# Warming products on a constant of ones, and three row transfers moved to GpSimd's queue

## The chip, the cores and the metric

One core of a Trainium2 chip runs the kernel. The time is the device time of one execution in microseconds, as the median of several runs. The profile is of one more execution of the same program.

## The reference

The inputs are x (2048 rows of 512), weights for an attention branch A and for a feed-forward branch B, and a gate vector. All is float32.

```
g = sigmoid(sum(x * gate_w, -1))
# A: linear attention, 32 heads of 16
q, k, v = split(x @ wqkv)
pq, pk = per head q @ w_phi, k @ w_phi
phi(p) = concat(softmax(p), softmax(-p))          # 32 features a head
kv = sum over rows of phi(pk)^T v;  z = sum over rows of phi(pk)
a = (phi(pq) kv / (phi(pq) z + 1e-6)) @ wo
# B: feed-forward, 1792 hidden
h = relu(x @ w1 + b1)^2
b = h @ w2 + b2
out = g * a + (1 - g) * b
```

## The kernel before

Every float32 product is made of three TensorE products of split operands: each operand is a high part (ScalarE copies it, rounded) and a low part (VectorE subtracts), as `split` (line 62) makes them, and `mm3` and `block` issue high by high and the two mixed terms.

The feed-forward branch sets the rhythm. The 14 hidden chunks are done in two sweeps of seven over four blocks of 512 rows; each step of the work list issues one `up` (12 products of 512 columns) and the `down` products of an earlier step. All other work is hung on slots between them: `at(slot, f, ...)` puts a function into a slot, two whole slots to a step, some 5 us each in the first sweep. The scheduler may issue ready work sooner; `tc.issue_after(ins)` pins what is traced in it behind `ins` in the order of that engine's queue, without a wait.

Start: `warm_up` (485) clears a tile `zeros` on VectorE and issues ten products of it into a PSUM bank that nobody reads; `start` (495) then fetches x's first block in four chunks and the weights of three hidden chunks, splits them and issues the first 36 true products in a fixed order (line 552). A first tiny ScalarE activation (`ready`, 521) reads `zeros` too.

The k and v projections of attention run in the first sweep as eight pairs of row chunks, one pair from slot 14 + 4.5 p on (`pair_steps`, 651), by a scheme of seven block products in place of eight. For pair p, `sums_load` (593) fetches two tiles of rows, 256 KB each and in runs of 512 bytes; `sums_add` (604) makes four sums in place, on GpSimd except for the first pair; `sums` (614) splits the result on ScalarE and VectorE. The weights of three of the seven blocks do not fit: they are kept in DRAM (`wkeep`) and come back in turn, 512 KB at a time, into three slots (two tiles `sloto`, one `slotez`), on ScalarE's queue (`again`, 626, issue shown as line 635) as soon as the products that read a slot are done.

`x_load` (564) fetches the next block's rows in four tiles of 256 KB, `x_split` (579) splits them later. These tiles and the halves of `sums_load` share one set of four buffers (`stage`, tag "in"), given out in the order of the code; a transfer waits until the low part of the tile that had the buffer before is made. Block 2 comes on GpSimd's queue, blocks 1, 3 and the return to block 0 (b = 4) on SyncE's through `load` (85). The halves of pair 4 (counted from 0) come on GpSimd's queue, all others on SyncE's.

GpSimd's queue holds, in the first sweep: writing the kept weights, part results to DRAM (901), some of the gate's row tiles (263), block 2's rows (570), the halves for pair 4 (600) and the additions (609 to 612). `st["summed"]` is the last of the latest additions, `st["stored"]` the latest store or halves' transfer behind which the next additions are pinned; `st["ahead"]` is the latest of SyncE's halves, behind which the gate's row tiles for blocks 2 and 3 are pinned.

Of the kernel before, what the change touches and what calls it, by code (L numbers as in the profile page):

```python
# [10 lines left out]
AF = mybir.ActivationFunctionType  # L11
# [5 lines left out]
P = 128  # L17
S, D, H, DH, F = 2048, 512, 32, 16, 1792
NK = D // P
SB = 512  # L20
NB = S // SB
# [14 lines left out]
def tile_gated_mix(ctx: ExitStack, tc: tile.TileContext, xT, xn, wqT, wkT, wphi, wv, wo, w1, b1, w2, b2, gw, out):  # L36
    nc = tc.nc
# [6 lines left out]
    work = pool("work", 2)  # L44
# [5 lines left out]
    def used(p):  # L50
        banks.remove(p)
        banks.append(p)
# [32 lines left out]
    def load(src, eng=nc.sync):  # L85
        t = stage.tile([P, 512], F32, tag="in", name="in")
        st["in"] = eng.dma_start(t, src)
        return t

    def row():  # L90
        return work.tile([P, D], F32, tag="row", name="row", bufs=6)

    def ffn_tiles(nm, fc):
        return (fpool.tile([P, 512], F32R, tag=nm + "h", name=f"{nm}h{fc}"),
                fpool.tile([P, 512], F32R, tag=nm + "l", name=f"{nm}l{fc}"))
# [25 lines left out]
    st, up_w, down_w = {}, {}, {}  # L121
# [137 lines left out]
    def gate_load(n):  # L259
        eng, pin = ((nc.sync, "in" if n > 1 else "wv"), (nc.gpsimd, "summed"), (nc.sync, "ahead"), (nc.sync, "ahead"))[n // NC]  # L260
        st["xn", n] = row()
        with tc.issue_after(st[pin].ins):
            st["xrow"] = eng.dma_start(st["xn", n], xn[n])
# [151 lines left out]
    def hidden(fc, ps):  # L415
        r = work.tile([P, SB], F32, tag="r", name="r")
        with tc.high_priority(offset=AHEAD):
            st["relu"] = nc.scalar.activation(r, ps, AF.Relu, bias=b1c[:, fc:fc + 1])  # L418
        nc.scalar.activation(r, r, AF.Square)  # L419
        hh = work.tile([P, SB], F32R, tag="hh", name="hh", bufs=LAG + 1)  # L420
        hl = work.tile([P, SB], F32R, tag="hl", name="hl", bufs=LAG + 1)
        st["act"] = split(r, hh, hl, nc.scalar, nc.vector)
        st["dve"] = st["lo"]
        return hh, hl
# [52 lines left out]
    def do_w1(fc):  # L477
        up_w[fc] = by_k(load_ffn("w1", w1[fc], fc))
# [4 lines left out]


    def warm_up():
        z = st["zeros"] = work.tile([P, 512], mybir.dt.bfloat16, tag="r", name="zeros")
        nc.vector.memset(z, 0.0)
        st["warm"] = ps_a.tile([P, 512], F32, tag="s", name="warm")
        idle(10)

    def idle(n):
        for _ in range(n):
            st["up"] = nc.tensor.matmul(st["warm"], st["zeros"][:, :P], st["zeros"], start=True, stop=True)


    def start():
        fs, wide = range(FIRST), FIRST * P
        W = [ffn_tiles("w1", f) for f in fs]
        ps = [p.tile([P, SB], F32, tag="s", name="u") for p in (ps_e, ps_b, ps_f)]
        xs = st["x", 0] = []  # L500
        for f in fs:
            up_w[f] = [tuple(z[:, P * f:P * (f + 1)] for z in W[k]) for k in range(NK - 1)]
            up_w[f].append(tuple(z[:, wide:] for z in W[f]))
        raw = [(stage.tile([P, 512], F32, tag="in", name="in"), row()) for _ in range(NK)]
        last = act = None

        def fetch(dst, src):
            nonlocal last
            with tc.issue_after(last.ins) if last else nullcontext():
                last = nc.sync.dma_start(dst, src)  # L510

        def first_w(k, a, b):
            return (raw[k][1][:, a * P:b * P].rearrange("p (f c) -> p f c", f=b - a),
                    w1[a:b, :, k * P:(k + 1) * P].rearrange("f p c -> p f c"))

        def follow(i, eng, *a):
            with tc.issue_after(i.ins) if i else nullcontext():
                return eng(*a)

        ready = small.tile([P, 1], F32, tag="den", name="ready", bufs=2)  # L520
        act = follow(nc.scalar.dma_start(*first_w(0, 0, 1)), nc.scalar.activation, ready, st["zeros"][:, :1], AF.Copy)
        for k in range(NK):
            fetch(raw[k][0], xT[0, :, k, :])
            fetch(*first_w(k, 0 if k else 1, FIRST))
        dve = None
        for k in range(NK):
            u, t = raw[k]
            xh, xl = (xpool.tile([P, SB], F32R, tag=g, name=f"{g}0_{k}") for g in ("xh", "xl"))
            xs.append((xh, xl))
            if k == 0:  # L530
                w = [(t[:, a:b], *(z[:, a:b] for z in W[k])) for a, b in ((0, P), (P, wide))]
            elif k < NK - 1:
                w = [(t[:, :wide], *(z[:, :wide] for z in W[k]))]
            else:
                w = [(t[:, P * f:P * (f + 1)], *(z[:, wide:] for z in W[f])) for f in fs]
            if k < 2:
                dve = follow(dve, nc.vector.tensor_copy, xh, u)
            else:
                act = follow(act, nc.scalar.activation, xh, u, AF.Copy)
            for src, hi, lo in w:  # L540
                act = follow(act, nc.scalar.activation, hi, src, AF.Copy)
            lows = [(lo, src, hi.bitcast(F32), ALU.subtract) for src, hi, lo in w]
            lows.insert(k == 0, (xl, u, xh.bitcast(F32), ALU.subtract))
            for x in lows:
                dve = follow(dve, nc.vector.tensor_tensor, *x)
            terms = [(f, 0, xh) for f in fs] + [(f, 0, xl) for f in fs] + [(f, 1, xh) for f in fs]
            if k == 0:
                terms.insert(1, terms.pop(6))
            if k == NK - 1:
                terms.sort(key=lambda x: x[0])  # L550
            for n, (f, part_, x) in enumerate(terms):
                st["up"] = follow(st["up"], lambda: nc.tensor.matmul(
                    ps[f], up_w[f][k][part_], x, start=k == 0 and (part_, x) == (0, xh),
                    stop=k == NK - 1 and part_ == 1))
        fetch(b1c, b1)
        do_w1(FIRST)
        for f in fs:
            hid[f] = hidden(f, ps[f])
            if f == 0:
                st["act0"] = st["act"]  # L560
        for p in (ps_e, ps_b, ps_f):
            used(p)

    def x_load(b):
        if b == 2:
            st["xin", b] = []
            for k in range(NK):
                with tc.issue_after(st["summed"].ins):
                    t = stage.tile([P, 512], F32, tag="in", name="in")
                    st["summed"] = nc.gpsimd.dma_start(t, xT[b, :, k, :])  # L570
                    st["xin", b].append(t)
                if k > 1:
                    gate_load(NC + k)
                    st["summed"] = st["xrow"]
        else:
            st["xin", b] = [load(xT[b % NB, :, k, :]) for k in range(NK)]
        st["x", b] = []

    def x_split(b, k):
# [13 lines left out]
    def sums_load(p):  # L593
        b, c = ROWS[p]
        rows = xT[b].rearrange("p k (h c r) -> p k h c r", h=2, c=2)[:, :, :, c, :]
        st["rows", p] = [stage.tile([P, 2, 2, P], F32, tag="in", name="in") for _ in range(2)]
        for i, t in enumerate(st["rows", p]):
            if p == 4:
                with tc.issue_after(st["stored"].ins):
                    st["stored"] = nc.gpsimd.dma_start(t, rows[:, 2 * i:2 * i + 2])  # L600
            else:
                st["ahead"] = nc.sync.dma_start(t, rows[:, 2 * i:2 * i + 2])
# [191 lines left out]
    for b in range(NB):  # L794
        for c in range(NC):
            s = b * SL + 2.5 * c - 1 if b > 1 else 17.5 + c / 2 if b else max(5.5, 3.5 + 2 * c)
            if b != 1 or c < 2:
                at(s, gate_load, b * NC + c)
            at(s + (4.5 if b == 1 else 3), gate_chunk, b * NC + c)
        if c == NC - 1:  # L800
            at(s + 4.5 if b == 1 else s + 3, gates, b)
        s, late = ((4, 2), (19.5, 1), (22, 2.5), (36, 2))[b]
        at(s, x_load, b + 1)
        for k in range(NK):
            at(s + late + k / 2, x_split, b + 1, k)
# [19 lines left out]
    for p in range(NB * NC // 2):  # L825
        n, s = 2 * p, 56.5 + 6 * p
        q, late = divmod(n, NC)[0], p == NB * NC // 2 - 1
# [31 lines left out]
    at(2, rows_alike, gwb, gw)  # L859
    at(2, rows_alike, b2b, b2)  # L860
    warm_up()
    start()
    with tc.issue_after(st["act0"].ins):
        for fc in range(LAG + 1):
# [84 lines left out]
```

## Time and profile before

| | |
|---|---|
| median of 3 runs | 507.90 us (507.86 to 508.17) |
| the profiled execution's own time | 508.57 us |
| its span, first to last instruction | 506.8 us |
| TensorE busy | 502.0 us, 99% |
| VectorE, ScalarE, GpSimd busy | 405.9, 256.2, 88.4 us |
| moved by DMA | 76.13 MB, 150 GB/s on the mean |

Product ends are modelled, so a busy share of 99% hides small stalls. They are seen in the distance between the starts of neighbouring products. In rows of the timeline the columns are start, duration, engine, line, operation, tile written and read, and in brackets the idle time before, with what ended it. A queue is marked with a q: SPq is SyncE's, ACTq ScalarE's; GpSimd's issues are shown as POOL DMA_DIRECT2D.

### The profile page before, as it was taken

How to read it: one execution, taken by the hardware profiler on the slowest of the kernel's cores; microseconds unless marked ns; L12 is line 12 of the kernel's file. 1: busy time of each engine (PE TensorE's matmuls, PEld its weight loads, DVE VectorE, ACT ScalarE, POOL GpSimd, SP SyncE). 2: the span in 40 equal slices, each digit the busy share in tenths (PEclk: the TensorE clock that was granted, in tenths of full speed). 3: DMA queues.
4: the chain of work that ended last, by engine and by line, in shares of the span. 5: the costliest groups of instructions: out<-in, count | busy, mean ns of one | idle time of the engine just before them, and what ended most of it. 6: DMA issues, size and time to landing. Idle time of an engine off the chain costs nothing.

```text
span 506.8 us, 9362 instructions
## 1 busy us (share of the span) xinstructions
PE 502.0 (99%) x3522; PEld 406.4 (80%) x3522; DVE 405.9 (80%) x679; ACT 256.2 (51%) x458; POOL 88.4 (17%) x103
## 2 busy tenths in 40 slices
PE   9999999999999999999999999999999999999997
PEld 5878788788888888888888877788787878788776
DVE  5569957998795979796898989897869797897824
ACT  4887655555263474454574745444456354333540
POOL 0000151204420025000013050211222221111200
PEclk9999999999999999999999999999999999999999
DMA  8858587756854578771375221325112231032102
GB/s 262 279 194 284 187 311 219 232 196 231 288 187 158 182 236 308 242 228 65 87 219 195 63 83 43 104 76 147 39 31 88 71 85 43 8 125 63 38 26 84
DMA packets 45861, 76.13 MB, mean 150 GB/s; under 512 B 6904, under 2 KB 23032, under 8 KB 45816
## 3 DMA queue, kind: packets, MB, share of 16 engines
q1 hardware_dynamic: 36104, 41.78, 26.7%
q10 hardware_dynamic: 6768, 23.79, 13.7%
q0 software_dynamic: 2944, 9.96, 5.4%
q8 instruction: 28, 0.46, 0.4%
q14 instruction: 17, 0.14, 0.1%
HBM read 57.68 MB, written 11.54 MB: 137 GB/s over the span
## 4 chain that ended last, share of the span: by engine, by line
PE 90%; DVE 6%; DMA 1%; POOL 1%; ACT 1%; issue 1%; DVEq 0%; POOLq 0%; ACTq 0%
PE d L77 9%; PE d L78 9%; PE d L79 9%; PE u L77 9%; PE u L78 8%; PE u L79 8%; PE pX L647 3%; PE att L79 3%; PE pX L649 3%; PE att L77 3%; PE att L78 3%; PE pX L648 3%; PE q L79 2%; PE q L78 2%; PE q L77 2%; PE pY L647 2%
## 5 line engine op out<-in xcount | busy, mean ns | idle before, releaser
L418 ACT ACTIVATE r<-u,b1c 128x512 f32<-128x512 f32 x56 | 38.5, 688 | 125.5 <-PE u L79 123.6
L77 PE MATMUL d<-w2h,hh 128*128 128x512 f32 x222 | 86.9, 391 | 0.0
L78 PE MATMUL d<-w2l,hh 128*128 128x512 f32 x222 | 86.5, 390 | 0.0
L79 PE MATMUL d<-w2h,hl 128*128 128x512 f32 x222 | 86.4, 389 | 0.0
L77 PE MATMUL u<-xh,w1h 128*128 128x512 f32 x212 | 83.7, 395 | 0.0
L78 PE MATMUL u<-xl,w1h 128*128 128x512 f32 x212 | 82.6, 390 | 0.0
L79 PE MATMUL u<-xh,w1l 128*128 128x512 f32 x212 | 82.5, 389 | 0.0
L333 POOL TENSOR_TENSOR ez<-e,z 128x512 f32<-128x512 f32 x32 | 43.1, 1370 | 166.6 <-ACT e L305 166.6
L67 DVE TENSOR_TENSOR hl<-r,hh 128x512 fp32r<-128x512 f32 x56 | 37.7, 674 | 24.7 <-ACT hh L64 24.7
L77 PEld LDWEIGHTS d<-w2h,hh 128*128 128x128 f32 x222 | 41.7, 188 | 9.2 <-issue 0.6
L78 PEld LDWEIGHTS d<-w2l,hh 128*128 128x128 f32 x222 | 41.7, 188 | 8.9 <-DVE w2l L67 0.4
L77 PEld LDWEIGHTS u<-xh,w1h 128*128 128x128 f32 x212 | 39.8, 188 | 11.1 <-issue 2.9
L79 PEld LDWEIGHTS d<-w2h,hl 128*128 128x128 f32 x222 | 41.7, 188 | 8.7
L79 PEld LDWEIGHTS u<-xh,w1l 128*128 128x128 f32 x212 | 39.8, 188 | 8.6 <-DVE w1l L67 0.2
L78 PEld LDWEIGHTS u<-xl,w1h 128*128 128x128 f32 x212 | 39.8, 188 | 7.9
L305 ACT ACTIVATE e<-e 128x1024 f32<-128x1024 f32 x27 | 28.6, 1059 | 25.2 <-DVE e L303 25.0
L308 DVE TENSOR_REDUCE sm<-e 128x64 f32<-128x1024 f32 x27 | 32.8, 1214 | 10.4 <-ACT e L305 10.4
L64 ACT ACTIVATE hh<-r 128x512 fp32r<-128x512 f32 x56 | 35.2, 628 | 1.1
L419 ACT ACTIVATE r<-r 128x512 f32<-128x512 f32 x56 | 35.0, 624 | 0.7
L686 ACT ACTIVATE tmp<-pX 128x512 f32<-128x512 f32 x24 | 14.4, 598 | 31.2 <-PE pX L649 27.6
L371 ACT ACTIVATE phiT<-tb 32x256 f32<-32x256 f32 x64 | 26.4, 412 | 6.1 <-DVE tb L356 5.1
L340 DVE TENSOR_REDUCE dz<-ez 128x64 f32<-128x1024 f32 x16 | 19.4, 1211 | 11.5 <-POOL ez L333 11.5
(184 smaller groups left out, 985.5 us busy)
## 6 DMA issues: line engine op xcount, KB each, us to landing
sloto<-wkeep ACTq DMA_DIRECT2D x30, 512.0 KB, 4.1
in<-in_xT SPq DMA_DIRECT2D x42, 256.0 KB, 4.2
slotez<-wkeep ACTq DMA_DIRECT2D x15, 512.0 KB, 4.6
phiT<-tb SPq DMA_DIRECT2D x192, 32.0 KB, 1.9
in<-in_w SPq DMA_DIRECT2D x23, 256.0 KB, 3.2
part<-row POOLq DMA_DIRECT2D x16, 256.0 KB, 5.2
row<-part SPq DMA_DIRECT2D x16, 256.0 KB, 2.7
out<-row SPq DMA_DIRECT2D x15, 256.0 KB, 2.2
```

The source lines that it names most:

```text
L64: i = nc.scalar.activation(hi, src, AF.Copy)
L67: st["lo"] = elo.tensor_tensor(lo, src, hi.bitcast(F32), ALU.subtract)
L77: nc.tensor.matmul(o, ah[:, sa], bh[:, sb], start=first, stop=False)
L78: nc.tensor.matmul(o, ah[:, sa], bl[:, sb], start=False, stop=False)
L79: return nc.tensor.matmul(o, al[:, sa], bh[:, sb], start=False, stop=last)
L305: nc.scalar.activation(ef, ef, AF.Exp)
L308: nc.vector.tensor_reduce(sm, e3, AX.X, ALU.add)
L333: nc.gpsimd.tensor_tensor(ez[:, hs, :], e3[:, hs, :], zbc[half], ALU.mult)
L371: nc.scalar.activation(dst, src, AF.Copy)
L418: st["relu"] = nc.scalar.activation(r, ps, AF.Relu, bias=b1c[:, fc:fc + 1])
L419: nc.scalar.activation(r, r, AF.Square)
L647: nc.tensor.matmul(ps, h, wh, start=first and j == 0, stop=False, skip_group_check=True)
```

## The change

The tile `zeros` and its memset go; the warming products and the tiny activation read a constant of ones that the program's preamble writes on GpSimd, one column read with step 0 as 512. There are eleven such products, not ten. Of block 3's rows, tile 1 is fetched on GpSimd's queue, pinned behind the latest additions (those of pair 2). The halves of pair 5 are fetched on GpSimd's queue, pinned behind the additions of pair 4, and pair 5's additions are pinned behind them.

```diff
     def warm_up():
-        z = st["zeros"] = work.tile([P, 512], mybir.dt.bfloat16, tag="r", name="zeros")
-        nc.vector.memset(z, 0.0)
+        st["ones"] = nc.const_aps.tensor(1.0, (P, 512), mybir.dt.bfloat16)
         st["warm"] = ps_a.tile([P, 512], F32, tag="s", name="warm")
-        idle(10)
+        idle(11)
 
     def idle(n):
         for _ in range(n):
-            st["up"] = nc.tensor.matmul(st["warm"], st["zeros"][:, :P], st["zeros"], start=True, stop=True)
+            st["up"] = nc.tensor.matmul(st["warm"], st["ones"][:, :P], st["ones"], start=True, stop=True)
...
-        act = follow(nc.scalar.dma_start(*first_w(0, 0, 1)), nc.scalar.activation, ready, st["zeros"][:, :1], AF.Copy)
+        act = follow(nc.scalar.dma_start(*first_w(0, 0, 1)), nc.scalar.activation, ready, st["ones"][:, :1], AF.Copy)
...
         else:
-            st["xin", b] = [load(xT[b % NB, :, k, :]) for k in range(NK)]
+            st["xin", b] = []
+            for k in range(NK):
+                late = b == 3 and k == 1
+                with tc.issue_after(st["summed"].ins) if late else nullcontext():
+                    st["xin", b].append(load(xT[b % NB, :, k, :], nc.gpsimd if late else nc.sync))
         st["x", b] = []
...
         for i, t in enumerate(st["rows", p]):
-            if p == 4:
-                with tc.issue_after(st["stored"].ins):
+            if p in (4, 5):
+                with tc.issue_after(st["stored" if p == 4 else "summed"].ins):
                     st["stored"] = nc.gpsimd.dma_start(t, rows[:, 2 * i:2 * i + 2])
             else:
                 st["ahead"] = nc.sync.dma_start(t, rows[:, 2 * i:2 * i + 2])
```

## Rows read from the trace of the kernel before

**Rows 1.** Page, part 1 (busy time, share, instructions) and part 4 (chain by engine).
```profile
PE 502.0 (99%) x3522; PEld 406.4 (80%) x3522; DVE 405.9 (80%) x679; ACT 256.2 (51%) x458; POOL 88.4 (17%) x103
...
PE 90%; DVE 6%; DMA 1%; POOL 1%; ACT 1%; issue 1%; DVEq 0%; POOLq 0%; ACTq 0%
```

**Rows 2.** Timeline of all engines from 0 to 22 us.
```profile
0.31 0.10 POOL L938 MEMSET const-bfloat16-1.0<- 128x1 bf16 x1
...
0.74 0.39 SPq L510 DMA_DIRECT2D in<-in_xT  x1
0.86 0.27 DVE L487 MEMSET zeros<- 128x256 uint32 x1 [0.86 <-PEq L938]
...
1.19 4.45 PE L493 MATMUL warm<-zeros 128*128 128x512 bf16 x10 [1.19 <-DVE zeros L487]
```

**Rows 3.** Timeline of TensorE alone, from 4.7 to 8.6 us.
```profile
5.35 0.78 PE L552 MATMUL u<-xh,w1h 128*128 128x512 f32 x1
5.93 0.63 PE L552 MATMUL u<-xh,w1l 128*128 128x512 f32 x1
...
6.78 0.48 PE L552 MATMUL u<-xh,w1h 128*128 128x512 f32 x1
7.10 0.85 PE L552 MATMUL u<-xl,w1h 128*128 128x512 f32 x3
...
8.24 0.62 PE L552 MATMUL u<-xh,w1h 128*128 128x512 f32 x2
```

**Rows 4.** Table by stretches: length, busy (count) of PE, PEld, DVE, ACT, POOL, PEclk, DMA, GB/s.
```profile
5.35:6.95 1.60, 1.60 (x5) 1.37 (x5) 1.52 (x4) 0.25 (x1) 0.00 (x0) 1.00 1.05 329
```

**Rows 5.** Timeline of ScalarE from 4.9 to 9 us.
```profile
4.98 0.63 ACT L518 ACTIVATE w1h<-row 128x128 fp32r<-128x128 f32 x2 [2.31 <-DMA row<-in_w]
7.28 0.53 ACT L518 ACTIVATE w1h<-row 128x384 fp32r<-128x384 f32 x1 [1.67 <-DMA row<-in_w]
```

**Rows 6.** Timeline of TensorE from 97.6 to 99.5 us.
```profile
98.10 0.39 PE L649 MATMUL pX<-sloto,xl 128*128 128x512 f32 x1
98.62 0.50 PE L647 MATMUL pX<-sloto,xh 128*128 128x512 f32 x1
```

**Rows 7.** View of line 635, its one issue at 91.7 us.
```profile
DMA to landing us min/median/max: 6.9/6.9/6.9
```

**Rows 8.** View of line 87, its one issue at 92.4 us.
```profile
DMA to landing us min/median/max: 6.5/6.5/6.5
```

**Rows 9.** Timeline of GpSimd from 93 to 143 us.
```profile
96.28 1.07 POOL L612 TENSOR_TENSOR in<-in 128x256 f32<-128x256 f32 x1
...
126.71 1.51 POOL L600 DMA_DIRECT2D in<-in_xT  x2
133.79 1.75 POOL L609 TENSOR_TENSOR in<-in 128x256 f32<-128x256 f32 x1 [5.57 <-DMA in<-in_xT]
...
138.63 0.74 POOL L609 TENSOR_TENSOR in<-in 128x256 f32<-128x256 f32 x1 [0.66 <-DMA in<-in_xT]
```

**Rows 10.** Timeline of ScalarE near 111 and 163 us: splits of block 3, pair 5.
```profile
111.35 1.66 ACT L64 ACTIVATE xh<-in 128x512 fp32r<-128x512 f32 x3
...
162.96 1.15 ACT L64 ACTIVATE sh<-in 128x512 fp32r<-128x512 f32 x2
```

**Rows 11.** Timeline of TensorE near 105.5 and 145 us: first readers of reloaded slots.
```profile
105.55 0.39 PE L647 MATMUL pX<-sloto,sh 128*128 128x512 f32 x1
...
145.12 0.39 PE L647 MATMUL pX<-sloto,xh 128*128 128x512 f32 x1
```

**Rows 12.** Timeline of ScalarE and its queue near 100 us.
```profile
99.64 0.33 ACTq L635 DMA_DIRECT2D sloto<-wkeep  x1
```

**Rows 13.** Views of line 635 (issues at 138.5, at 130.5) and of line 570.
```profile
DMA to landing us min/median/max: 3.3/3.3/3.3
DMA to landing us min/median/max: 7.8/7.8/7.8
DMA to landing us min/median/max: 3.7/6.0/6.8
```

## The prediction

> **What bounds the kernel now.** Start with the page's busy line and its chain of waits: TensorE is busy for 502.0 of 506.8 us and carries 90% of the chain [rows 1]. So a microsecond is won only where TensorE stands still or runs below its pace, and the reader should look for those places in TensorE's own rows, by the distance from one product's start to the next, not by the busy time (product ends are modelled, so a stall barely shows as idle time). The common product, 512 columns, comes every 0.23 us: from 7.10 to 8.24 us five of them pass [rows 3]. The change touches two places where the distance is longer. The first is the start: no product before 1.19 us, and the first true ones 0.43 us apart [rows 2, 3]. The second is one product of the third pair's first block: 0.52 us from 98.10 to 98.62 [rows 6].
>
> **The start: the memset removed.** The first warming product waits for VectorE's memset of the zeros, 0.86 + 0.27 = 1.13 us, and starts at 1.19 [rows 2]. The ones are a constant that GpSimd has written at 0.31 + 0.10 = 0.41 us, ahead of the opening barrier, so nothing is left to wait for. When TensorE begins then, no row shows; SyncE's first work after that barrier is at 0.74 and VectorE's at 0.86 [rows 2]. I take the middle, 0.80: 0.39 us earlier, with bounds of 0.33 and 0.45. Nobody else wanted the memset: ScalarE's tiny first activation reads it too, but behind a table load.
>
> **The eleventh product.** In the cold stretch a product takes 0.43 us (5.93 to 6.78 is two of them [rows 3]). Ten from 1.19 occupy TensorE to about 5.46; eleven from 0.80 to about 5.50, and from 0.86 to 5.56. That is 0.04 to 0.10 us later. The first true product cannot start much earlier in any case: its weights come from ScalarE's split, which began at 4.98 when the DMA had landed [rows 5]. And the second true product comes 0.58 us after the first [rows 3], 0.15 more than the pace, so it waits for its own operand and the 0.04 to 0.10 vanish there. Worth of the earlier start as such: 0.
>
> **The clock.** The granted-clock column says 1.00 for the stretch from 5.35 to 6.95 us [rows 4], but the distances tell more: 0.43 us for 512 columns is 1.2 GHz, 0.23 is the upper level of 2.4 with a little overhead. The distance 6.78 to 7.10 is 0.32, a mixture, which puts the rise at about 6.97 us, 5.78 us after TensorE's first product, which kept it busy all that time [rows 2, 3]. Each microsecond by which the rise comes earlier saves 1 - 0.23/0.43 = 0.47 us, as long as operands are there. If the rise follows the first product, it comes 0.39 us earlier: 0.39 x 0.47 = **0.18 us**. From below it is bounded by 0 (the rise stays where it is; nothing that the change does makes TensorE less busy before it). From above, by the next operand: TensorE reaches the second chunk of the rows at 8.24 us [rows 3], and that chunk's weights are split by ScalarE from 7.28 to 7.81, after waiting for a DMA [rows 5], so no more than 8.24 - 7.81 = 0.43 us can be gained. Behind that TensorE runs without a pause and ScalarE waits for it, so what is won here is carried to the end. I take 0.18, since the warming stretch moves as a whole.
>
> **The tile of rows.** At 98.10 the distance is 0.52 instead of 0.23: 0.295 us lost (0.522 - 0.227) [rows 6]. The product waits for a kept weight (sloto from wkeep, 512 KB on ScalarE's queue), issued at 91.7, landed 6.9 us later, at 98.6 [rows 7]; it was wanted at 98.10 + 0.23 = 98.33, so 6.6 us after the issue. Beside it ran tile 1 of the fourth block's rows: 256 KB on SyncE's queue, issued 92.4 and landed 6.5 us later [rows 8], in the air for the whole of that time. The change pins this tile behind the third pair's last addition on GpSimd, which ends at 96.28 + 1.07 = 97.35 [rows 9]. With nothing new beside it, the same kind of load lands after 3.3 us at 138.5 [rows 13]. The truth lies between 3.3 and 6.9; every value below 6.6 saves the whole **0.295 us**. I take the whole, since 0.3 us of 6.9 is little against 256 KB removed; tile 0, issued just before it, and the second kept weight stay, so the bound from below is 0.
>
> The Trainium skill (Trainium Kernel Development and Optimization, Key Constraints) says that DMAs from SyncE, ScalarE and GpSimd all run on the same 16 engines, and that several issuing engines save issue time alone. By that rule the change of queue is worth nothing, and the sum without the tile would be 507.7. No run here shows the queue changed alone; what I count on is the issue 5 us later.
>
> **What the tile costs there.** GpSimd's own loads of these rows landed 3.7 to 6.8 us after the issue [rows 13], so the tile is there at 101.1 to 104.2. ScalarE splits tiles 1 to 3 from 111.35 [rows 10]: at least 7 us of slack. On GpSimd only the next pair's additions are queued behind the issue, and SyncE fetches their rows no sooner than these tiles' buffers come free again. The tile's buffer had come free at 92.4, when SyncE filled it. Tiles 2 and 3 take the buffers that come free later, in the same order. Cost 0, except for company of the next kept weight (a rival, below).
>
> **The sixth pair's halves.** They leave SyncE's queue and go behind the fifth pair's additions, which end 0.66 us before 138.63, at 137.97 [rows 9]. Two such issues took 1.51 us on GpSimd, and their data came 5.57 us after that, when the additions started [rows 9]; so the sixth pair's additions begin at 137.97 + 1.51 + 5.57 = 145.1 instead of 138.63, and end some 3.6 us later, at 148.7. ScalarE reads the result at 162.96 [rows 10]: 14 us of cover. No product waits in this stretch today, so nothing is gained either. SyncE's next row tile, queued behind the halves today, can go earlier; its reader, the gate, is off the path. Worth 0.
>
> **Sum.** 0.18 + 0.295 = 0.47. The profiled execution took 508.57 (span 506.8 and 1.8 around it), 0.67 above the median of the runs, 507.90; it would come to 508.1, and the median to **507.4**.
>
> **Rivals.**
> (a) The clock's rise stays at 6.97 whatever TensorE does before. For it: 5.78 us of unbroken products went by before the rise, and a start 0.39 us earlier need not be what it waits for. Time 507.90 - 0.30 = 507.6.
> The Trainium skill (TensorE: Matmul & The Clock Gate, Part 1) supports this one: the monitor runs freely and is not restarted by the kernel. One trace cannot show it.
> (b) The longer warming brings the rise ahead of the first true product; then the cap counts: 507.90 - 0.43 - 0.30 = 507.2. Against it: the products from 1.19 on did not do it.
> (c) The tile was not what made the kept weight late; tile 0 and the other kept weight were. Then only 0.18 is won: 507.7.
> (d) Slower: the moved transfers hold up the *next* kept weight. Place: the load issued at 99.64 [rows 12], read at 105.55 [rows 11], 5.9 us of room; tile 1 now travels just ahead of it, beside tile 2. A kept weight issued at 130.5, among rows on two queues, took 7.8 us [rows 13]. That would be 1.9 us late, and 507.4 + 1.9 = 509.3. It outweighs the gain from a landing of 5.9 + 0.5 = 6.4 us on. The same may happen to the load of 138.5 (read at 145.12 [rows 11], 6.6 us of room), which now has the halves beside it: at 7.8 us, 1.2 late, 508.6. Against it: only 3.3 us were needed there, and the halves that crowded 130.5 are the ones taken away.
> (e) Slower: an operand that is one column read 512 times may feed TensorE slower; no row shows such a product. At half the pace eleven take 4.7 us more: about 512.
>
> **How the numbers follow.** Forecast 0.48 (507.4); (a) 0.21 (507.6); (b) 0.09 (507.2); (c) 0.08 (507.7); (d) 0.10 (508.0 to 509.3); (e), or another order of the queues that opens a wait as large, 0.04. A measurement of this kernel tells from no change what exceeds about 0.2%, 1.0 us. Below 506.9 lies only an extreme of (b) with luck in the medians: 0.05. Above 508.9 lie half of (d), (e) and a little for what I overlooked: 0.11. The same: 0.84. The range runs from 506.9 to 508.7, which leaves out (e), the upper part of (d) and that extreme.
>
> **What would show it.** Right: the first warming product at 0.74 to 0.86; first true product at about 5.35; the distance falling from 0.43 to 0.23 at about 6.6 us (a: at 6.97; b: before 5.35); 0.23 instead of 0.52 before the second product of that block, near 98; tile 1 issued by GpSimd near 97; the sixth pair's additions near 145. Wrong: a distance over 0.23 near 105 or 145, a first true product after 5.6, or VectorE and ScalarE in another order around the splits.

## The result, and the profile after

The changed kernel took 508.67 us (median of 22 runs, 507.71 to 509.15) beside 507.85 us for the kernel before (22 runs on the same chip): a ratio of 1.0015, interval 1.0009 to 1.0022, or 0.82 us slower. Forecast were 507.4 us and a small gain. The difference stays within 0.2%, as the largest of the three chances had it, but its sign is the other one and its interval does not reach zero; the time lies at the upper edge of the range (508.7).

The profiled execution of after took 508.79 us with a span of 507.0, that of before 508.57 with 506.8. The page's busy line and chain by engine, which answer to [rows 1]:

```profile
PE 501.9 (99%) x3523; PEld 405.8 (80%) x3523; DVE 404.9 (80%) x678; ACT 256.5 (51%) x458; POOL 89.9 (18%) x106
...
PE 85%; DVE 8%; DMA 2%; ACT 1%; issue 1%; POOL 1%; SPq 0%; DVEq 0%; ACTq 0%; POOLq 0%
```

One product more on TensorE, one instruction fewer on VectorE, three more on GpSimd, as the diff says. In the chain, TensorE's 90% have become 85, and VectorE (8%) and DMA (2%) have gained: somewhere the end now hangs on them. TensorE's timeline of after at the start, which answers to [rows 2, 3]:

```profile
0.78 4.40 PE L492 MATMUL warm<-const-bfloat16-1.0 128*128 128x512 bf16 x11 [0.78 <-PEq L941]
5.37 0.50 PE L551 MATMUL u<-xh,w1h 128*128 128x512 f32 x1 [0.19 <-ACT w1h L517]
5.71 0.49 PE L551 MATMUL u<-xh,w1l 128*128 128x512 f32 x1
...
8.05 0.96 PE L551 MATMUL u<-xh,w1h 128*128 128x512 f32 x3 [0.24 <-ACT w1h L517]
```

The first warming product starts at 0.78 in place of 1.19, the first true one at 5.37 as before, and the second chunk is reached at 8.05 in place of 8.24, after a wait for ScalarE's w1h. So 0.19 us were won there. TensorE's timeline of after around the third pair's first block (98) and its reloaded slot (105), answering to [rows 6, 11]:

```profile
98.04 0.39 PE L650 MATMUL pX<-sloto,xh 128*128 128x512 f32 x1
98.26 0.39 PE L651 MATMUL pX<-sloto,xh 128*128 128x512 f32 x1
...
105.52 0.46 PE L650 MATMUL pX<-sloto,sh 128*128 128x512 f32 x1
105.81 0.40 PE L651 MATMUL pX<-sloto,sh 128*128 128x512 f32 x1
```

The stall at 98 is gone, and only 0.07 us was lost near 105. GpSimd's timeline of after, answering to [rows 9]:

```profile
98.92 0.55 POOL L87 DMA_DIRECT2D in<-in_xT  x1
...
137.98 1.51 POOL L603 DMA_DIRECT2D in<-in_xT  x2
144.21 0.74 POOL L612 TENSOR_TENSOR in<-in 128x256 f32<-128x256 f32 x1 [4.73 <-DMA in<-in_xT]
```

The tile goes out at 98.92, the sixth pair's halves at 137.98, and that pair's additions start at 144.21; ScalarE reads their result at 163.01, as late as before, and no product waits there.

So every place that the prediction looked at went as it said or nearly so (the tile goes out 1.6 us later than expected, as these additions began at 95.14 in place of 93.52, waiting for their rows), and the kernel is slower. TensorE's timeline shows where, first of before and then of after, at the second block of the first pair:

```profile
57.75 0.39 PE L77 MATMUL u<-xh,w1h 128*128 128x512 f32 x1
57.98 0.50 PE L647 MATMUL pX<-slotez,sh 128*128 128x512 f32 x1
```

```profile
57.74 0.39 PE L77 MATMUL u<-xh,w1h 128*128 128x512 f32 x1
58.38 0.50 PE L650 MATMUL pX<-slotez,sh 128*128 128x512 f32 x1 [0.25 <-ACT sh L64]
```

The distance is 0.23 in before and 0.64 in after: a new wait of 0.41 us. The chain of waits of after, from 36 to 58.6 us, tells what it hangs on (start, duration, what):

```profile
36.79 5.91 DMA in<-in_w
42.69 0.02 issue
42.71 0.04 ACT w2h L64
42.76 0.49 issue
43.25 0.63 ACT sloto L64
43.88 0.02 issue
43.90 0.69 DVE sloto L67
...
57.32 0.35 DVE in L614
57.67 0.02 issue
57.69 0.64 ACT sh L64
58.33 0.04 issue
58.38 0.50 PE pX L650
```

A tile of w2, issued by SyncE at 36.79, lands after 5.91 us; ScalarE's split of it starts at 42.71; from 43.90 on VectorE works nearly without a gap up to 57.67, when the operand of the product at 58 can be rounded. VectorE, not TensorE, is the bound of this stretch whenever that tile is late. In before the same split started at 42.31, and nothing waited; its row in ScalarE's timeline:

```profile
42.31 0.63 ACT L64 ACTIVATE w2h<-in 128x512 fp32r<-128x512 f32 x1 [1.01 <-DMA in<-in_w]
```

The two profiled spans differ by 0.24 us. By places: the second chunk 0.19 earlier (of it 0.07 left at the next products, as the one behind a wait came 0.34 later, not 0.23, and 0.01 at 57.74), the new wait at 58 +0.41, the stall at 98 -0.41 (the 0.30 and 0.11 at the product behind it), near 105 +0.07, after the last product +0.18. The medians differ by more than the profiles, as the profiled execution of before lies 0.7 above its own median.

### The profile page after: what moved, and what is told of

Read it like the earlier page. It is cut to its first block, busy times and chain, and to the rows that moved or that the text cites. A ratio compares the mean times of both kernels' runs of the same rounds, so it can differ in the third digit from the quotient of the medians.

```text
span 507.0 us, 9360 instructions
## 1 busy us (share of the span) xinstructions
PE 501.9 (99%) x3523; PEld 405.8 (80%) x3523; DVE 404.9 (80%) x678; ACT 256.5 (51%) x458; POOL 89.9 (18%) x106
## 4 chain that ended last, share of the span: by engine, by line
PE 85%; DVE 8%; DMA 2%; ACT 1%; issue 1%; POOL 1%; SPq 0%; DVEq 0%; ACTq 0%; POOLq 0%
PE d L77 8%; PE d L78 8%; PE d L79 8%; PE u L77 8%; PE u L78 8%; PE u L79 8%; PE pX L650 3%; PE att L79 3%; PE pX L652 3%; PE att L77 3%; PE att L78 3%; PE pX L651 3%; PE q L79 2%; PE q L78 2%; PE q L77 2%; PE pY L651 2%
```

## The experiments

The first theory was that of the traces above: the opening wins 0.2 us, a wait at 58 us takes it back, and the rest is chance. Its rivals: the moved transfers cost the time (by company for other loads), or the missing memset does (by what it shifts). Letters in the expectations are explained in each. All kernels were run beside the kernel before on the same chip. One table holds what all of them showed; the wait columns are distances between products beyond the pace of 0.227 us, in the one profiled execution of each. The ratios given below are worked out from all single runs and not from the two medians, so the two can differ in sign where a difference is within the noise, as for e1. "Clock" is when the granted clock rises to its upper level by the trace's clock records, "2nd" when TensorE reaches the second chunk. "Fetch", "store" and "weights" are explained with the third group of experiments.

```
kernel memset moved | clock  2nd  | fetch store weights | waits at: 58   98   105  305 | median, before's, difference
before yes   -      |  6.95  8.24 | 37.2  4.10  5.48    |         0.00 0.30 0.00 0.34 |
after  no    all    |  4.58  8.05 | 39.5  3.11  5.93    |         0.41 0.00 0.07 0.34 | 508.67 507.85 +0.82
e1     no    -      |  4.23  7.68 | 39.2  3.10  5.90    |         0.42 0.25 0.00 0.34 | 508.03 508.11 -0.08
e2     yes   tile   |  6.72  8.14 | 37.6  4.14  5.79    |         0.29 0.00 0.04 0.00 | 508.46 508.11 +0.35
e3     yes   halves |  5.40  7.83 | 38.1  4.19  5.89    |         0.36 0.00 0.00 0.37 | 508.24 508.11 +0.13
e4     no    -      |  4.14  7.48 | 39.2  3.11  5.81    |         0.24 0.08 0.00 0.00 | 508.39 508.11 +0.28
e5     yes   -      |  5.96  7.79 | 36.8  4.01  5.40    |         0.00 0.00 0.32 0.00 | 508.01 508.33 -0.32
e6     no    all    |  3.90  7.73 | 39.8  3.10  5.92    |         0.39 0.00 0.25 0.00 | 508.65 508.33 +0.32
e7     yes   all    |  7.15  8.35 | 37.3  4.15  5.33    |         0.00 0.00 0.61 0.34 | 508.38 508.33 +0.05
e8     yes   -      |  3.85  7.86 | 36.9  3.64  5.33    |         0.00 0.00 0.00 0.00 | 508.04 508.33 -0.29
e9     yes   -      |  3.62  7.84 | 37.4  4.18  5.30    |         0.00 0.08 0.00 0.00 | 507.97 508.18 -0.21
e10    yes   (gate) |  4.58  8.09 | 37.7  4.18  5.35    |         0.00 0.00 0.54 0.00 | 508.67 508.18 +0.49
e11    no    (gate) |  5.91  7.86 | 40.4  3.67  5.81    |         0.31 0.00 0.76 0.34 | 508.85 508.18 +0.67
e12    no    all    |  3.44  7.64 | 42.0  3.09  5.16    |         0.00 0.00 0.57 0.34 | 508.96 508.18 +0.78
e13    yes   all    |  6.21  7.93 | 37.5  3.66  5.32    |         0.00 0.00 0.00 0.00 | 507.93 507.71 +0.22
e15    no    -      |  3.67  8.07 | 39.2  3.09  5.79    |         0.28 0.00 0.00 0.34 | 508.40 507.71 +0.69
e16    yes   -      |  3.56  7.82 | 36.9  3.78  5.31    |         0.00 0.00 0.00 0.34 | 507.69 507.71 -0.02
e17    no    all    |  5.38  7.72 | 39.1  3.10  5.74    |         0.23 0.00 0.06 0.35 | 508.46 507.71 +0.75
```

### The parts alone

e1 has the opening alone (ones, eleven products, no memset), e2 the tile alone, e3 the halves alone, e4 the opening with ten products.

```diff
-        z = st["zeros"] = work.tile([P, 512], mybir.dt.bfloat16, tag="r", name="zeros")
-        nc.vector.memset(z, 0.0)
+        st["ones"] = nc.const_aps.tensor(1.0, (P, 512), mybir.dt.bfloat16)
...
-        idle(10)
+        idle(11)      # e1; e4 keeps idle(10); the readers follow in both
```
```diff
+                late = b == 3 and k == 1      # e2
...
-            if p == 4:
+            if p in (4, 5):                   # e3
```

> The kernel before with the opening part of the change alone: the ones in place of the zeros, eleven products. Theory A (the opening costs: what is gained at the clock's rise is lost again where DMAs end the wait, and more): 508.4 to 508.8, about 0.8 over before, as the whole change. Theory B (the moved transfers cost, the opening is worth what was forecast): 507.5 to 507.8, 0 to 0.3 under before.

> The kernel before with tile 1 of block 3 alone on GpSimd's queue. Theory A: 507.6 to 507.9, at most 0.3 under before, since the 0.3 us stall near 98 us goes and nothing else changes. Theory B: 508.1 to 508.6, with a new distance over 0.23 us between products near 105 us.

> The kernel before with the sixth pair's halves alone on GpSimd's queue. Theory A: 507.7 to 508.0, no difference. Theory B: 508.1 to 508.6, with a new distance over 0.23 us between products from 138 us on.

> The opening part with ten products in place of eleven, the transfers as before. Theory A: if the cost lies in the eleventh product, 507.6 to 507.9; if in the earlier start, as the run with eleven, 508.4 to 508.8. Theory B: 507.5 to 507.8, as the run with eleven.

Ratios: e1 1.0007 (0.9998 to 1.0017), e2 1.0011 (1.0002 to 1.0020), e3 1.0008 (0.9998 to 1.0017), e4 1.0009 (1.0000 to 1.0017). No part is faster. Of the intervals e2's alone lies clear of 1, but its trace waits 0.29 at 58, far ahead of the place where its tile was moved. Neither theory's times fit all four (they were set beside 507.9 for the kernel before, and it took 508.11 on this chip), and the new distances that theory B named near 105 in e2 and from 138 us on in e3 are 0.04 and nothing. What the traces say is worth more. In e3 and e4 the tile is not moved, and the stall at 98 is (all but) gone all the same: it is not there in every execution. And e1 and e4, the two without the memset, both wait at 58; so do e2 and e3, with it.

### The same again, and the start made late

e5 is the kernel before once more and e6 the changed kernel once more, no edit in either. e7 moves all three transfers and leaves the opening alone. e8 is the kernel before with three more warming products.

```diff
-        idle(10)
+        idle(13)      # e8 alone
```

> The kernel before itself, nothing changed, as a second program. Theory C (each part alone came out 0.05 to 0.35 us over before, also a part that the trace gives no cost; a program set beside before is measured that much slower): 0.2 to 0.5 us over before. Theories A and B: within 0.2 us of before. In its trace, by theory D (the time at the start of the first pair's second block, near 58 us, is set by DMAs and falls anywhere in 57.5 to 58.8), that product between these bounds.

> The whole change once more, beside the others on the same chip. If the 0.8 us of the first comparison belong to the change: 0.6 to 1.0 over before. If single parts add up (their medians: -0.1, +0.35, +0.1): 0.2 to 0.5 over. Theory C: 0.2 to 0.5 over, as the kernel before again.

> Both moves of transfers, the opening as before. Theory B: 0.5 to 0.9 over before, as the whole change. Theory A: within 0.2 of before. Theory C: 0.2 to 0.5 over, as the kernel before again.

> The kernel before with thirteen warming products, so that TensorE is free for true products some 1.3 us later (about 6.7 us) and reaches the second chunk of rows some 0.5 us later. Prediction's step (a shift at the start is carried to the end): 0.5 us over before, and the product near 58 us as much later. Theory D (near 58 us TensorE waits for DMAs in any case): 0 to 0.2 over, TensorE some 0.5 late until 57 us and 0 to 0.2 behind it.

Ratios: e5 0.9995 (0.9986 to 1.0004), e6 1.0005 (0.9995 to 1.0016), e7 0.9998 (0.9989 to 1.0008), e8 0.9995 (0.9983 to 1.0008). The three transfers together cost nothing that can be told from zero with the memset in place (e7). e5, the kernel before again, came out 0.32 under it, which leaves theory C without support. e6 is 0.32 over before, where 0.6 to 1.0 was expected if the 0.8 belonged to the change. e8 did not do what it was meant for. Its first products:

```profile
1.19 4.27 PE L493 MATMUL warm<-zeros 128*128 128x512 bf16 x13 [1.19 <-DVE zeros L487]
5.37 0.48 PE L552 MATMUL u<-xh,w1h 128*128 128x512 f32 x1
```

The clock rose at 3.85, so thirteen products were over as early as ten in before, and TensorE reached the second chunk 0.38 earlier, not 0.5 later: in its trace e8 is no test of a late start. Over the 18 traces the rise lies between 3.44 and 7.15; with ten products of zeros alone, the very same opening, it came at 6.95, 6.72, 5.40, 5.96, 7.15 and 4.58. The Trainium skill (TensorE: Matmul & The Clock Gate, Part 1) has the monitor running freely, not started by the kernel's first product; this spread agrees with it.

e5 and e7 also show what the third pair does. The tile's move sets no stall aside for good; where the one at 98 is missing, the same pair can lose as much at the slot that is reloaded next. TensorE's timeline of e7:

```profile
105.70 0.50 PE L651 MATMUL pX<-sloto,sh 128*128 128x512 f32 x1 [0.45 <-DMA sloto<-wkeep]
```

This is 0.61 us lost (distance 0.83 from 104.87) for a kept weight issued at 100.37. It stands in e6, e7 and e12 with the tile moved, but in e5, e10 and e11 without it too, and in e13 and e2, with it, not at all or for 0.04.

### The gate's rows out of the way, and the memset put back

By now the new wait at 58 was the lead: the tile of w2 lands 5.7 to 5.9 us after its issue in after, e1, e4 and e6, and after 5.3 to 5.5 in before, e5, e7 and e8 (column "weights": from SyncE's issue to ScalarE's split). Beside it travel the gate's row tiles, which are issued behind it, and two stores of kept weights that GpSimd issues just ahead. A third candidate is in the page's part 3, which lists instructions as users of the DMA queues; for after:

```profile
q8 instruction: 28, 0.46, 0.4%
q14 instruction: 17, 0.14, 0.1%
```

The trace's DMA records give each of these a start: "fetch" in the table is the second of q14's transfers of 8 KB after the start-up. It begins at 36.8 to 38.1 us in all ten kernels with the memset, and at 39.1 or later in all eight without. "Store" is the time to landing of the first of the two stores.

e9 is e1 with an unread memset put back; e10 is the kernel before with the gate's row tiles of chunks 2 and 3 issued ahead of that w2 tile, e11 the same with e1's opening; e12 is the changed kernel a third time.

```diff
+        nc.vector.memset(work.tile([P, 512], mybir.dt.bfloat16, tag="r", name="unread"), 0.0)
         st["ones"] = nc.const_aps.tensor(1.0, (P, 512), mybir.dt.bfloat16)      # e9
...
-                at(s, gate_load, b * NC + c)
+                at(s if b or c < 2 else 6.5, gate_load, b * NC + c)             # e10, e11
```

> The opening part (ones, eleven products) with VectorE's memset kept, of a tile that nobody reads; transfers as before. Theory E (without the memset a fetch of instructions on queue 14 falls at 39.2 to 39.8 us instead of 36.8 to 38.1 and the weight tile issued near 36.5 lands 5.9 us after its issue instead of 5.3 to 5.8): the fetch back at 36.8 to 38.1, the landing at 5.3 to 5.8. Rival (the earlier pace of TensorE does it): fetch and landing as in the runs with ones, 39.2 to 39.8 and 5.9. In both, theory D: the product near 58 us starts 15.67 us after ScalarE's split of that tile, or without a wait.

> The kernel before with two of the gate's row tiles (chunks 2 and 3) issued ahead of the weight tile of 36.8 us, in the quiet time near 33 us, instead of behind it. Theory D (transfers between 36 and 43 us set the product near 58 us): the weight tile lands 4 to 5 us after its issue, no wait near 58 us; 0 to 0.3 under before. Prediction's step (no wait there that counts): no difference.

> The same with the opening part of the change (ones, eleven products), transfers otherwise as before. Theory D: no wait near 58 us, so the earlier clock is kept: TensorE there at 57.3 to 57.7, time 0.3 to 0.6 under before. If the opening costs in another way (theory A): at or over before.

> The whole change a third time. If its cost is about 0.1 from traces (opening 0, the stall near 98 gone, a new one near 105) and the first comparison fell high: 0 to 0.4 over before. If 0.8 belongs to it: 0.6 to 1.0 over. In the trace a wait of 0.07 to 0.6 us near 105.

Ratios: e9 0.9994 (0.9982 to 1.0007), e10 1.0004 (0.9992 to 1.0015), e11 1.0006 (0.9994 to 1.0018), e12 1.0010 (0.9999 to 1.0022). The gate's rows are not it: with them ahead, w2 takes the same 5.35 with the memset and 5.81 without, where theory D expected 4 to 5, and e11 still waits. The memset is the better candidate: e9 has the fetch back at 37.4, w2 after 5.30 and no wait at 58. Who gives way to whom is seen in the stores, in the views of GpSimd's store line, its one issue near 35.5; before, after and e12 in turn:

```profile
DMA to landing us min/median/max: 4.1/4.1/4.1
```

```profile
DMA to landing us min/median/max: 3.1/3.1/3.1
```

```profile
DMA to landing us min/median/max: 3.1/3.1/3.1
```

and of SyncE's load of w2 (line 87, its one issue near 36.5), after and e12:

```profile
DMA to landing us min/median/max: 5.9/5.9/5.9
```

```profile
DMA to landing us min/median/max: 5.1/5.1/5.1
```

With the memset the first store takes 3.6 to 4.2 us and w2 mostly 5.3 to 5.5; without it the store takes 3.1 (3.7 in e11) and w2 5.7 to 5.9. It looks as if 0.5 to 1 us were shifted from a store that nobody waits for to a load on which VectorE's next 14 us hang. e12 fits: its fetches came at 34.0 and 42.0, so none lay beside the store or w2, and both the store (3.1) and w2 (5.1) are fast. There the fetch of 34.0 lay beside the weights issued at 32.0, which took 4.25 us (2.6 to 3.3 for such loads near 32 us in the other traces); TensorE's timeline and the chain of e12:

```profile
36.97 0.50 PE L77 MATMUL u<-xh,w1h 128*128 128x512 f32 x1 [0.95 <-ACT w1h L64]
```

```profile
32.02 4.25 DMA in<-in_w
```

That is 1.11 us lost, 21 us earlier than in the other traces. e2 and e3 don't fit: memset, fetch at 37.6 and 38.1, a slow store, and a slow w2 too. So the fetch's place is the likely carrier, which 16 of 18 traces bear out; that an 8 KB transfer as such makes the load late was not tried by itself, and the records don't say which of the 16 DMA engines, or whose instructions, it was. In e9, as in e13 and e16 below, the memset comes back together with its tile, so that it is the instruction and not the tile is argued, not shown: the late load goes to a tile of another tag.

### The whole change with the memset, and the opening with and without

e13 is the changed kernel with the unread memset put back, e15 is e1 and e16 is e9 once more, e17 the changed kernel a fourth time.

```diff
+        nc.vector.memset(work.tile([P, 512], mybir.dt.bfloat16, tag="r", name="unread"), 0.0)      # e13, e16
         st["ones"] = nc.const_aps.tensor(1.0, (P, 512), mybir.dt.bfloat16)
```

> The whole change with VectorE's memset kept (nobody reads it). Theory E (taking the memset out moves a fetch of instructions from about 37 us to 39 to 40.5 us, beside the weight tile that ScalarE's split near 42 waits for): the fetch is back before 38.2 us, the weight tile lands 5.2 to 5.5 us after its issue, that split starts by 42.4, no product waits at 58, and the time is 0.2 to 0.6 us under that of the whole change run beside it. Rival M (the three moved transfers cost it): as slow as the whole change, 0.3 to 0.8 us over the kernel before. Rival N (chance places near 98, 105 and 305 us make the difference): no fixed order; the medians differ by the sum of those places in the profiles.

> The opening alone once more (ones, eleven products, no memset; no transfer moved). Theory E: the fetch at 39 to 40.5 us, the weight tile 5.7 to 5.9 us after its issue, a wait of 0.2 to 0.5 us at 58; time 0 to 0.4 us over the kernel before. Rival M: no difference from the kernel before, or the 0.2 us that the earlier start wins.

> The opening alone with the unread memset kept, once more. Theory E: the fetch before 38.2 us, no wait at 58, 0.1 to 0.4 us under the opening alone run beside it. Rival M and N: as the opening alone within 0.1 us, or either sign.

> The whole change a fourth time, beside its version with the memset kept. All theories: 0.3 to 0.8 us over the kernel before. Theory E: fetch at 39 to 40.5 us, a wait at 58 of 0.2 to 0.6 us. Rival N: no wait at 58 needed; the difference sits in the places near 98, 105 and 305 us.

Without the memset: e15 508.40, ratio 1.0012 (1.0004 to 1.0021), and e17 508.46, ratio 1.0014 (1.0005 to 1.0022). With it: e16 507.69, ratio 0.9998 (0.9989 to 1.0006), and e13 507.93, ratio 1.0002 (0.9994 to 1.0011). An instruction whose result nobody reads makes the kernel 0.71 us (e15 less e16) and 0.53 us (e17 less e13) faster, and takes away the wait at 58 both times. Worked out from the single runs, the means of these pairs are 0.67 us (interval 0.36 to 0.97) and 0.48 us (0.19 to 0.74) apart; 0.1 to 0.4 was expected of the first and 0.2 to 0.6 of the second. ScalarE's timeline of e15 and of e16, the split of that w2 tile:

```profile
42.60 0.63 ACT L64 ACTIVATE w2h<-in 128x512 fp32r<-128x512 f32 x1 [1.85 <-DMA in<-in_w]
```

```profile
41.91 0.63 ACT L64 ACTIVATE w2h<-in 128x512 fp32r<-128x512 f32 x1 [1.16 <-DMA in<-in_w]
```

And TensorE's timeline of e15 and of e16, around the first product of the block at 58:

```profile
57.76 0.39 PE L77 MATMUL u<-xh,w1h 128*128 128x512 f32 x1
58.26 0.50 PE L646 MATMUL pX<-slotez,sh 128*128 128x512 f32 x1
```

```profile
57.53 0.39 PE L77 MATMUL u<-xh,w1h 128*128 128x512 f32 x1
57.76 0.47 PE L647 MATMUL pX<-slotez,sh 128*128 128x512 f32 x1
```

All 18 kernels issue their true products in the same order, so how far one trace lags another can be read at each product. From the last product ahead of the block at 58 to those near 61 us, e15 loses 0.45 us to e16, e17 0.42 to e13, after 0.41 to before, e11 0.40 to e10, e6 0.57 to e7 and e12, where w2 came early, nothing to e9. So the traces put some 0.4 us of the difference at the wait at 58. The rest between e15 and e16 is 0.23 from the start. Between e17 and e13 it is a sum of chances: e13 loses 0.57 near 28, e17 0.17 near 105 and 0.51 at 305. Two more pairs on one chip differ by the opening: e11 is 0.18 over e10 and e6 0.27 over e7, which runs that spread over 2 us and more can't tell from zero.

Over all comparisons, the kernels without the memset lie 0.53 us above the kernel before on the mean (eight: +0.82, -0.08, +0.28, +0.32, +0.67, +0.78, +0.69, +0.75), those with it 0.04 (nine). A fit to all single runs with one term for each edit and one for each chip's level gives 0.30 us for the missing memset (0.16 to 0.45), 0.27 for the tile (0.07 to 0.49) and 0.09 for the halves (-0.13 to 0.30). The intervals are too narrow: the same code, e1 and e15, came out at -0.08 and +0.69 on two chips (ratios 1.0007 and 1.0012). So the memset's share is shown, by two pairs on one chip and the place in their traces; the tile's is not, as e7 and e13, which have it, are level with the kernel before.

## Why the prediction was right or wrong

**What bounds the kernel.** Right for the start, 98 and the whole, and incomplete: TensorE's share of the chain hid that the stretch from 44 to 58 us has VectorE as a second bound, at no distance. In before, the product at 57.98 followed at TensorE's pace, so the rows showed no wait, and the prediction looked only where the distance was longer than the pace. ScalarE's w2 split at 42.31 plus 15.67 us gives 57.98: in before the two paths met to within 0.01 us. In the nine traces that wait there (after, e1, e2, e3, e4, e6, e11, e15 and e17) the product starts 15.66 to 15.67 us behind that split each time, as VectorE works nearly without a gap in between.

**The memset removed; the failed step.** "Nobody else wanted the memset" holds for data, so its removal was given no cost. It cost 0.4 us or so at 58 us: the median wait there is 0.30 in the eight traces without it and 0 in the ten with it. That no product depended on the memset was no reason for no effect. What changed with it, as far as the runs show, is when the second fetch of instructions came (36.8 to 38.1 us with it, 39.1 to 42.0 without) and how late w2 landed (5.3 to 5.5 us in eight of ten, 5.7 to 5.9 in seven of eight). Why one instruction moves the fetch by some 2 us, and whether the fetch is what holds w2 up, stays open.

**The start.** The first warming product at 0.78 (0.80 taken), the first true product at 5.37 (5.35 expected): right. **The clock**: it rose at 4.58, neither at 6.6 as forecast nor at 6.97 as rival (a) had it, but ahead of the first true product, which is rival (b). Its cap was right in kind, the wait for ScalarE's w1h at the second chunk, with 0.19 us in place of 0.43 as the split came only at 7.47. One trace says little of the change, as the rise wandered by 2.6 us with the opening of before. The 17 traces with ten or eleven products say more: the rise comes at 4.42 on the mean in the eleven with ones and at 6.13 in the six with ten products of zeros, and TensorE is 0.23 us further on at 9 us, near the 0.18 of the forecast though not by its count of 0.39 us. (e8, zeros and thirteen products, rose at 3.85.) The estimate of 6.97 for before agrees with the clock's record, 6.95.

**"What is won here is carried to the end"**: wrong for the changed kernel. 0.19 us were won at 8.05, 0.01 was left at 57.74, and the wait at 58 would have taken the rest: e1 leads before by 0.43 us on its way to the block at 58, and by 0.04 at 61. Elsewhere the step holds: what a trace has won or lost at 9 us it still has at 27, to within 0.06, and e5, e8, e9 and e16, where w2 comes in time, lead before by 0.22 to 0.36 on the way to 58 and by 0.39 to 0.48 at 61.

**The tile of rows**: the stall at 98 went, as said, and the tile's own landing was early enough (issued 98.92, 3.4 us to landing). In this pair of traces it was worth 0.41 us, more than the 0.295, as the product behind the stall came late too. But it wasn't a steady loss. 0.25 to 0.30 stand in only two (before and e1) of the 11 traces where the tile isn't moved. A term taken from one execution was counted in full where its mean over these was 0.06 us. Rival (d), the next kept weight held up, came true in part: 0.07 here, 0.25, 0.57 and 0.61 in e6, e12 and e7; but 0.32, 0.54 and 0.76 in kernels without the move make that chance as well, and it is not what made after slow. The waits at 98 and 105 together are 0.23 us on the mean in the seven traces with the tile moved and 0.21 in the eleven without.

**The halves**: right. Additions at 144.21 (145.1 expected), nobody waits. **The operand with step 0**, rival (e): eleven products in 4.40 us, no slower than zeros.

**The sum.** Forecast -0.47; measured +0.82 in this comparison and +0.32, +0.78 and +0.75 in three more. The gain at the start is 0.01 ahead of 58 in place of 0.18, the tile's gain isn't there in the mean of the traces in place of 0.295, and the missing memset costs some 0.4 by the traces and 0.5 to 0.7 by the pairs, for which the sum had no term. What else makes up the 0.82 isn't shown: with one trace of each kernel, waits of 0.3 to 0.8 us that come and go can't be told apart in it.

## What to carry to other kernels

Before a gain at the start is carried to the end, look for the products that arrive just in time: follow each long chain on VectorE or ScalarE back to its load, add it up, and ask by how much it would have to slip to be seen; a place with a margin of 0.01 us is a bound, though no row shows a wait. A stall seen in one execution of a kernel whose DMA queues are full is a sample, and is to be counted by how often it comes. And an instruction taken out or put in can shift when instructions are fetched and loads land, far from its own place, so an edit of one small instruction wants a control with the instruction kept and its result unread.

## What the hardware showed beyond that

**Instructions are fetched by the DMA engines while the kernel runs.** The 8 KB transfers of q14 near 35 to 42 us took 0.3 to 1.1 us each by the DMA records, and the second of them moved by some 2 us with one memset of VectorE.

**A race of 10 ns.** Near 300 us VectorE and GpSimd each start an operation of two inputs, within 0.01 us of each other. VectorE's timeline of before and of e13, and GpSimd's of both:

```profile
300.14 2.36 DVE L314 TENSOR_TENSOR e<-e,w 128x1024 f32<-128x1024 f32 x1
```

```profile
299.92 1.22 DVE L314 TENSOR_TENSOR e<-e,w 128x1024 f32<-128x1024 f32 x1
```

```profile
300.13 3.52 POOL L333 TENSOR_TENSOR ez<-e,z 128x512 f32<-128x512 f32 x2 [5.79 <-ACT e L305]
```

```profile
299.91 3.64 POOL L333 TENSOR_TENSOR ez<-e,z 128x512 f32<-128x512 f32 x2 [5.79 <-ACT e L305]
```

VectorE's operation takes 2.36 us in the one and 1.22 in the other. The records give starts in whole ns: GpSimd's lies 6 to 10 ns ahead of VectorE's in all ten traces with the 2.36, and 3 to 5 ns ahead in the eight others. In those it is GpSimd's first operation of the two that is longer, 2.39 us in place of 1.29. TensorE pays at 305; its timeline of before:

```profile
305.82 0.50 PE L79 MATMUL att<-woh,o 128*128 128x512 f32 x1 [0.18 <-DVE o L67]
```

0.34 us or a little more are lost there in ten of the 18 traces, six of the eight without the memset and four of the ten with it. The Trainium skill (SBUF — State Buffer, Who interferes with whom) has the two engines share a port that one of them holds for a whole instruction, when VectorE reads two inputs and GpSimd reads too; the doubled time agrees. Such draws can make up the difference between two executions: e5 and before are the same program, and e5's last product comes 0.73 us earlier: 0.36 us were won ahead of 58, 0.42 at 98 and 0.47 at 305, 0.46 were lost near 105, and little elsewhere.
